# Earlier weights, shorter setup and back-to-back row scatters in a block-sorted attention followed by a routed expert layer

## The chip, the cores and the metric

The kernel runs on one core of one Trainium2 chip. The core has TensorE (PE in the profile; its weight loads are PEld), VectorE (DVE), ScalarE (ACT), GpSimd (POOL) and SyncE (SP), each with its own instruction stream, run in program order. Sixteen DMA engines move data between main memory (HBM) and on-chip memory (SBUF); DMAs are issued here from the POOL queue (software) and the SP queue (hardware). The metric is the device time of one execution in microseconds (us). Before the change it is 233.02 us, the median of three runs (231.26 to 235.55). The profiled execution took 233.46 us, of which the span from the first to the last instruction is 231.7 us.

## The reference

Attention over 4 batches, 8 heads, 768 positions and 64 dimensions. Keys and values are first mixed between 8 blocks of 96 positions by a matrix P (8x8 for each batch and head) that five rounds of row and column normalisation make; each query block attends only to its own sorted block. The output becomes 3072 rows of 512, and every row goes to one of 8 experts, its own best one.

```python
P = sort_net
for _ in range(5):
    P = exp(P - max(P, -1)); P /= sum(P, -1); P /= sum(P, -2)
k_sorted = einsum('bhij,bhjcd->bhicd', P, k_b)      # the same for v
attn = softmax(scale * q_b @ k_sorted_b.T) ; out = attn @ v_sorted_b
x = out.transpose(0, 2, 1, 3).reshape(3072, 512)
logits = x @ w_gate + modality_bias[modality_id]
e_idx = argmax(logits, 1) ; gate_w = softmax(logits)[row, e_idx]
for e in range(8):                                   # w1: 512x1024, w2: 1024x512
    mask = e_idx == e
    out[mask] = gate_w[mask, None] * (relu(x[mask] @ w1[e]) @ w2[e])
```

## The kernel before

The attention is cut into 32 units u = 0 to 31. A unit has one head of a pair of batches (g = u // 16) and half of its blocks. Eight units make a chunk m of 768 rows. When a chunk is complete its rows are gated (`gate_T`, `gate_L`), an expert is chosen for each (`choose`), a place in a scratch tensor in HBM is worked out (`place`, whose first matmuls are called rk in the trace), and eight indirect DMAs of 96 rows each scatter them to that place (`one(t)`). `table(m)` then makes the row addresses of the expert slots of 256 rows that are filled, and the slot's rows are read back, transposed (`xT`), by SP. Slots 0 and 1 become ready with chunk 0, slots 2 and 3 with chunk 1, slots 4 to 7 with chunk 2, slots 8 to 12 with chunk 3. The expert work of a slot is made of "pieces": four of `mL1` (8 matmuls each, hp in the trace) and two of `mL2` (8 matmuls each, yp), whose results leave by an indirect DMA (`y_out`, 25 of them). Even slots use weight buffer 0, odd slots weight buffer 1.

The issue order is fixed by hand. Setup and loads, with cuts:

```python
load_q(0, 0)            # POOL: four heads of q, two DMAs
... iota, identity ...
load_k(0, 0); load_k(0, 1); load_v(0); load_q(0, 1)
spread_q(0, 0, nc.gpsimd); spread_q(0, 1, nc.gpsimd)   # two copies each on POOL
for u in range(4): tq_pe(u)                            # PE transposes of q
...                                                    # five rounds of P; make_bd(0)
for f, g, x0, kd in g0[:8]: f(g, x0, kd)               # sort k of g = 0
scores(0); expo(0)
home_pick(); home_map(); mod_rows()                    # DVE chains, one PE transpose (modT)
load_k(1, 0); load_k(1, 1)
wait_w = gate_consts()                                 # five operations on POOL
make_bd(1)                                             # one PE matmul (rep), three DVE operations
scores(1); expo(1)
late_consts()                                          # eight DVE operations
for n, (f, g, x0, kd) in enumerate(g0[8:]): f(g, x0, kd)   # sort v of g = 0 (va)
load_v(1); load_q(1, 0); load_q(1, 1)
zero_block(); av(0); wait_w(); prep_s(4)
```

The main loop, and what is hung on its units:

```python
at2(9, place, 0)                          # issues scatter 0 of chunk 0
for t in range(1, 8):
    at1(9 + t, lambda t: ones_[0](t), t)  # scatters 1 to 7, one for each unit
    if t == 3: at1(9 + t, lambda: load_w(0, parts=(0,)))
at1(16, table_x, 0)                       # table, then the reads of the slots
at1(16, lambda: load_w(0, parts=(1,))); at1(16, lambda: load_w(1))
at1(18, place, 1) ... at2(24, table_x, 1)
at1(26, place, 2) ... at1(31, table_x, 2)
def pace(u): return (0, 0) if u < 18 else (1, u % 2)   # pieces of a unit
for u in range(2, 32):
    p1, p2 = pace(u)
    scores(u); expo(u)
    for f, a in A1.get(u, []): f(*a)      # at1
    run_pieces(p1)
    av(u - 1); prep_q(u + 2); prep_s(u + 3)
    for f, a in A2.get(u, []): f(*a)      # at2
    run_pieces(p2)
run_pieces(1); av(31); run_pieces(2); gate_T(3, 3); run_pieces(1)
gate_L(3, 3); choose(3); run_pieces(2); place(3)
for t in range(1, 8):
    run_pieces(2); ones_[3](t)
table_x(3); run_pieces(1000)
```

Each scatter after the first of a chunk also waits for the ScalarE or VectorE instruction that `mark[0]` names, so that the rows "leave at an even pace":

```python
ins = nc.gpsimd.indirect_dma_start(out=xs_dram, ...)
after = [mark[0].ins] if t else []
for pre in after:
    tc.add_manual_dep(ins.ins, pre.name, SYNC, reason="rows leave at an even pace")
```

Of the kernel before, what the change touches and what calls it, by code (L numbers as in the profile page):

```python
# [17 lines left out]
def kernel(  # L18
# [72 lines left out]
    def q_in(g, hh):  # L91
        base = q_in1 if g else v_sb[1].rearrange("p x d -> p (x d)")
        return base[:, hh * 3072:(hh + 1) * 3072]
# [19 lines left out]
    def load_v(g):  # L113
        nc.gpsimd.dma_start(out=v_in, in_=v_src[g * 128:(g + 1) * 128])

    def load_q(g, hh):
        t = q_in(g, hh).rearrange("p (r h f) -> p r h f", r=2, h=4)
        return [nc.gpsimd.dma_start(out=t[:, par], in_=q[2 * g + par, 4 * hh:4 * hh + 4]
                                    .rearrange("h (p t) d -> p h (t d)", t=6)) for par in range(2)][0]

    def spread_q(g, hq, eng=None):
        t = q_in(g, hq // 2).rearrange("p (r h t d) -> p r h t d", r=2, h=4, t=6)
        il = q_il[hq % 2].rearrange("p (h t r d) -> p h t r d", h=2, t=6, r=2)
        for z in range(2):
            (eng or nc.vector).tensor_copy(il[:, z], t[:, :, (hq % 2) * 2 + z].rearrange("p r t d -> p t r d"))  # L125
# [1 line left out]
    sI = singles.tile([128, 32], I32)  # L127
    pI = singles.tile([128, 1], I32)
    idI = singles.tile([BLK, NTL], I32)
    load_q(0, 0)  # L130
    nc.gpsimd.iota(sI, pattern=[[1, 32]], base=0, channel_multiplier=0)
    make_identity(nc, ident)
    load_k(0, 0)
    load_k(0, 1)
    load_v(0)
    load_q(0, 1)
    jI = singles.tile([1, 4], I32)
    hI = singles.tile([1, 4], I32)
    nc.gpsimd.iota(pI, pattern=[[0, 1]], base=0, channel_multiplier=1)
# [1 line left out]
    nc.gpsimd.iota(jI, pattern=[[1, 2], [0, 2]], base=0, channel_multiplier=0)  # L141
    nc.gpsimd.iota(hI, pattern=[[PR, 2], [CAP, 2]], base=0, channel_multiplier=0)
    spread_q(0, 0, nc.gpsimd)
    spread_q(0, 1, nc.gpsimd)

    ones_bf = singles.tile([128, 128], BF16)
    ones8 = singles.tile([128, E], FP32)
# [40 lines left out]
    def perm_mult(dst, srcs, nm):  # L188
        eng = nc.gpsimd if nm == "w" else nc.vector
        tmp = small.tile([128, 4, E, E], FP32, tag="ptmp", name=f"ptmp{nm}")  # L190
        a = bass.AP(tensor=srcs.tensor, offset=srcs.offset, ap=[srcs.ap[0], srcs.ap[1], [0, E], srcs.ap[2]])
        p_ = bass.AP(tensor=perm.tensor, offset=perm.offset, ap=[perm.ap[0], [0, 4], perm.ap[1], perm.ap[2]])
        eng.tensor_tensor(tmp, a, p_, ALU.mult)
        return lambda: nc.vector.tensor_reduce(dst, tmp, AX.X, ALU.add)
# [39 lines left out]
    def tq_out(u, eng):  # L234
        g, h = u // 16, u % 8
        qT = qTb[g][:, h * 768:(h + 1) * 768].rearrange("p (i t r) -> p i t r", i=NB, t=6)
        eng(qT, tq.pop(u).rearrange("p t (i r) -> p i t r", r=16))

    for u in range(4):
        tq_pe(u)  # L240
    for it in range(5):
        if it == 0:
            nc.vector.tensor_reduce(red, P_t, AX.X, ALU.max)
            nc.vector.tensor_tensor(P_t, P_t, red.broadcast_to([BH, NB, NB]), ALU.subtract)
        nc.scalar.activation(P_t, P_t, ACT.Exp)
        if it == 3:
            tq_out(0, nc.scalar.copy)
        if it == 4:
            for u in range(1, 4):
                tq_out(u, nc.scalar.copy)  # L250
        for f in gap[it]:
            f()
        nc.vector.tensor_reduce(red, P_t, AX.X, ALU.add)
        nc.vector.reciprocal(red, red)
        nc.vector.tensor_tensor(P_t, P_t, red.broadcast_to([BH, NB, NB]), ALU.mult)
        nc.vector.tensor_reduce(red, P_swap, AX.X, ALU.add)
        nc.vector.reciprocal(red, red)
        colb = bass.AP(tensor=red.tensor, offset=red.offset,
                       ap=[red.ap[0], [0, NB], red.ap[1]])
        nc.vector.tensor_tensor(P_bf if it == 4 else P_t, P_t, colb, ALU.mult)  # L260
# [40 lines left out]

    wgf = small.tile([128, 4, E], FP32, tag="wgf", name="wgf")

    def gate_consts():
        red_w = perm_mult(wgf, wg_sb, "w")
        nc.gpsimd.tensor_scalar(modN, modF, -1.0, 1.0, ALU.mult, ALU.add)

        def bb(r):
            t = BTp[0:BLK, r]
            return bass.AP(tensor=t.tensor, offset=t.offset, ap=[t.ap[0], [0, NTL], t.ap[1]])  # L310
        tmp = small.tile([BLK, NTL, E], FP32, tag="btmp", name="btmp")
        nc.gpsimd.tensor_tensor(biasm, modF.broadcast_to([BLK, NTL, E]), bb(1), ALU.mult)
        nc.gpsimd.tensor_tensor(tmp, modN.broadcast_to([BLK, NTL, E]), bb(0), ALU.mult)
        nc.gpsimd.tensor_tensor(biasm, biasm, tmp, ALU.add)

        def rest_w():
            red_w()
            nc.vector.tensor_copy(wgp, wgf)
        return rest_w

    busy = [0.0, 0.0]

# [54 lines left out]
        return u // 16, (u // 8) % 2, u % 8  # L377

    def prep_s(u):
        if 4 <= u < 32 and not (u // 8) % 2 and u % 2 == 0:  # L380
            spread_q(u // 16, (u % 8) // 2)
            use(dve=0.7)

    def prep_q(u):
        if 4 <= u < 32 and not (u // 8) % 2:
            tq_pe(u)
            tq_out(u, nc.scalar.copy if pick(0.8, 0.56) else nc.vector.tensor_copy)

# [85 lines left out]
    def place(m):  # L474
# [32 lines left out]
        def one(t):  # L507
            if t:
                nc.gpsimd.nop()
            ins = nc.gpsimd.indirect_dma_start(  # L510
                out=xs_dram, out_offset=bass.IndirectOffsetOnAxis(ap=dest[:, t:t + 1], axis=0),
                in_=xt.bitcast(I32)[:, t], in_offset=None)
            after = [mark[0].ins] if t else []
            tc.declare_no_dep(ins.ins, group="xs", reason="rows are disjoint", **({"keep": after} if after else {}))
            tc.add_to_no_dep_group("xs", ins.ins)
            for pre in after:
                tc.add_manual_dep(ins.ins, pre.name, SYNC, reason="rows leave at an even pace")
            scat[m].append(ins.ins)
        ones_[m] = one
        one(0)  # L520
        nxt = ohs[(m + 1) % 2]
        ohsum = small.tile([BLK, E], FP32, tag="ohsum", name=f"ohsum{m}")
        nc.vector.tensor_reduce(ohsum, oh.rearrange("p t e -> p e t"), AX.X, ALU.add)
# [73 lines left out]
    def zero_block():  # L597
        ins = nc.sync.dma_start(out=xs_dram[ZR:ZR + PR].rearrange("(t p) w -> p t w", t=2), in_=zsrc2)
        in_xs_group(ins.ins)
        pads.append(ins.ins)  # L600
# [8 lines left out]
    def w_views(z):  # L609
        o = z * WCOL  # L610
        return (w01[:, o:o + 4 * F].rearrange("p (c f) -> p c f", c=4),
                w01[:, o + 4 * F:o + WCOL].rearrange("p (c f) -> p c f", c=8))

    def load_w(z, tab=None, n=None, parts=(0, 1)):
        tb, n = (etab, z) if tab is None else (tab, n)
        er = nc.values_load(tb[0:1, n:n + 1], engines=(PoolEng,), min_val=0, max_val=E - 1)
        v1, v2 = w_views(z)
        if 0 in parts:
            nc.gpsimd.dma_start(out=v1, in_=moe_w1[bass.ds(er, 1)].rearrange("o (c p) f -> p (o c) f", p=128))
        if 1 in parts:  # L620
            nc.gpsimd.dma_start(out=v2, in_=moe_w2[bass.ds(er, 1)].rearrange("o (c p) f -> p (o c) f", p=128))

    def stage_of(s):
        return 0 if s < 2 else 1 if s < 4 else 2 if s < 8 else 3
# [123 lines left out]
    expo(0)  # L748
    home_pick()
    home_map()  # L750
    mod_rows()
    load_k(1, 0)
    load_k(1, 1)
    wait_w = gate_consts()
    make_bd(1)
    scores(1)
    expo(1)
    late_consts()
    use(dve=-busy[1], act=-busy[0])
    for n, (f, g, x0, kd) in enumerate(g0[8:]):  # L760
        f(g, x0, kd)
    load_v(1)
    load_q(1, 0)
    load_q(1, 1)
    zero_block()
    av(0)
    wait_w()
    prep_s(4)

    st = {"tab": -1, "x": 0, "l1": 0, "done": 0, "pos": 0}  # L770

# [24 lines left out]
    def at2(u, f, *a):  # L796
        A2.setdefault(u, []).append((f, a))

    at2(8, lambda: nc.vector.memset(v_sb[1][:, :, D:D + 1], 1.0))
    for m in range(4):  # L800
        for c in range(4):
# [3 lines left out]
                at2(u, gate_L, m, c)  # L805
        if m < 3:
            at2(8 * m + 9, choose, m)
    at2(9, place, 0)
    for t in range(1, 8):
        at1(9 + t, lambda t: ones_[0](t), t)  # L810
        if t == 3:
            at1(9 + t, lambda: load_w(0, parts=(0,)))
    at1(16, table_x, 0)
    at1(16, lambda: load_w(0, parts=(1,)))
    at1(16, lambda: load_w(1))
    at1(18, place, 1)
    for t in range(1, 8):
        at2(17 + t, lambda t: ones_[1](t), t)
    at2(24, table_x, 1)
    at1(26, place, 2)  # L820
    for t in range(1, 8):
        (at2 if t % 2 else at1)(27 + t // 2, lambda t: ones_[2](t), t)
    at1(31, table_x, 2)
    k_at = [5] * 3 + [6] * 3 + [7] * 3 + [8, 9, 10]
    v_at = [10, 11, 11, 11, 12, 12, 12, 13, 13, 13, 14, 14, 14, 15, 15, 15]
    for u, (f, g, x0, kd) in zip(k_at + v_at, jobs(1, [m_] * 28)):
# [34 lines left out]
    for u in range(2, 32):  # L861
        p1, p2 = pace(u)
        scores(u)
        expo(u)
        for f, a in A1.get(u, []):
            f(*a)
        run_pieces(p1)
        av(u - 1)
        prep_q(u + 2)
        prep_s(u + 3)  # L870
        for f, a in A2.get(u, []):
            f(*a)
        run_pieces(p2)
    run_pieces(1)
    av(31)
    run_pieces(2)
    gate_T(3, 3)
    run_pieces(1)
    gate_L(3, 3)
    choose(3)  # L880
    run_pieces(2)
    place(3)
    for t in range(1, 8):
        run_pieces(2)
        ones_[3](t)
    table_x(3)
    run_pieces(1000)
    assert st["pos"] == len(pieces)
# [74 lines left out]
```

## Time and profile before

| what | before |
|---|---|
| time, median of 3 | 233.02 us |
| span of the profiled execution | 231.7 us |
| busy PE, DVE, ACT, POOL | 164.9, 104.7, 94.3, 76.1 us |
| mean granted TensorE clock | 0.846 |
| last matmul of the expert work starts at | 216.00 us |
| HBM read, written | 27.35, 10.52 MB |

The page has six parts. Its second part cuts the span into 40 slices of 5.8 us and gives the busy share of each engine in tenths, the granted TensorE clock (PEclk) and the DMA share. The chain of waits goes back from the last instruction, at each step to what released it; read forward it is a list of start, length and what was on the path. The list of waits tells which engine stood still for whom: total us, times, longest. A timeline lists one engine's instructions in order of time; in brackets stands the idle time before an instruction and what ended it. A table of windows gives, for stretches of 4 us, the busy us of each engine with its instructions (x), the granted clock (1.00 is full), the DMA share and the GB/s moved.

### The profile page before, as it was taken

The numbers are of one execution on the slowest core, as the hardware profiler recorded it, in microseconds if no ns is written. First come the engines' busy times: TensorE is split into PE (matmuls) and PEld (weight loads), VectorE is DVE, ScalarE is ACT, GpSimd is POOL, SyncE is SP. The second block draws the span as 40 slices with busy tenths as digits, with TensorE's granted clock in tenths as the row PEclk, the third lists the DMA queues.
The fourth block names the chain that finished last, engine by engine and source line by source line (L and its number), as shares of the span: only waits on it lengthen the run. The fifth ranks groups of instructions, "written<-read, shape, count | busy, mean of one in ns | idle before, by whom it ended". The sixth has DMA issues, their size and how long they took to land.

```text
span 231.7 us, 5104 instructions
## 1 busy us (share of the span) xinstructions
PE 164.9 (71%) x2023; PEld 122.8 (53%) x2023; DVE 104.7 (45%) x340; ACT 94.3 (41%) x147; POOL 76.1 (33%) x102
## 2 busy tenths in 40 slices
PE   0265667995999600298889888999990999999600
PEld 0154565985889500286565657668660576674200
DVE  5868866657548660044566436233270133232100
ACT  2264445665577710075464626443341132322300
POOL 7621515000434420031633465337651031333300
PEclk9997587569569955569999999999998699999965
DMA  5999999990119399981215323594364642212200
GB/s 69 208 228 203 218 213 174 198 184 3 36 36 162 101 150 184 191 138 37 108 48 129 97 75 121 127 145 148 96 214 97 105 103 96 92 45 91 89 15 0
DMA packets 30129, 27.67 MB, mean 119 GB/s; under 512 B 18799, under 2 KB 25743, under 8 KB 29840
## 3 DMA queue, kind: packets, MB, share of 16 engines
q0 software_dynamic: 11760, 23.10, 45.7%
q1 hardware_dynamic: 18336, 4.16, 11.8%
q8 instruction: 18, 0.29, 0.6%
q14 instruction: 15, 0.12, 0.2%
HBM read 27.35 MB, written 10.52 MB: 163 GB/s over the span
## 4 chain that ended last, share of the span: by engine, by line
PE 54%; DVE 16%; DMA 13%; issue 5%; POOL 3%; ACT 2%; SPq 1%; POOLq 0%; DVEq 0%
PE hp L663 19%; PE yp L686 15%; DMA xT<-xs_scratch 10%; PE ka L349 3%; PE gt L433 3%; DVE xb L424 3%; PE va L358 3%; PE op L420 3%; PE sc L401 2%; PE lg L439 2%; DMA xs_scratch<-zpad 2%; PE tq L231 1%; POOL xs_scratch L510 1%; DMA xs_scratch<-xb,dest 1%; DVE v_sb L336 1%
## 5 line engine op out<-in xcount | busy, mean ns | idle before, releaser
L663 PE MATMUL hp<-xT,w 128*128 128x256 bf16 x384 | 50.1, 284 | 18.5 <-DMA xT<-xs_scratch 18.4
L510 POOL DMA_INDIRECT xs_scratch<-xb,dest x32 | 29.6, 925 | 68.5 <-issue 33.6
L663 PEld LDWEIGHTS <-w 128*128 128x128 bf16 x384 | 37.6, 102 | 27.1 <-issue 12.6
L677 POOL DMA_INDIRECT out_dram<-kvb,idg x25 | 24.6, 985 | 54.5 <-ACT kvb L673 27.3
L407 ACT ACTIVATE attnT<-sc 96x768 bf16<-96x768 f32 x32 | 25.8, 806 | 10.8 <-PE sc L401 10.6
L657 ACT ACTIVATE hT<-hp 128x512 bf16<-128x512 f32 x17 | 10.1, 596 | 35.7 <-PE hp L663 35.6
L686 PE MATMUL yp<-w,qT 128*128 128x512 bf16 x96 | 22.9, 383 | 0.0
L424 DVE TENSOR_TENSOR xb<-op,rs 96x512 bf16<-96x512 f32 x32 | 22.0, 687 | 1.7 <-DMA xs_scratch<-xb,dest 0.6
L686 PE MATMUL yp<-w,hT 128*128 128x512 bf16 x96 | 22.5, 379 | 0.0
L423 DVE RECIPROCAL rs<-op 96x8 f32<-96x8 f32 x32 | 6.4, 199 | 30.5 <-PE op L420 29.1
L673 ACT ACTIVATE kvb<-yp,idg 128x512 f32<-128x512 f32 x15 | 10.3, 687 | 21.5 <-PE yp L686 21.5
L231 PE MATMUL tq<-ident,q_il 128*128 128x128 bf16 x96 | 10.8, 270 | 10.7 <-POOL q_il L125 10.3
L420 PE MATMUL op<-v_sb,attnT 96*128 96x65 bf16 x256 | 15.1, 207 | 2.1 <-DVE v_sb L336 1.3
L358 PE MATMUL va<-bd,kvb 128*128 128x128 bf16 x128 | 14.6, 285 | 1.4 <-ACT v_sb L336 0.8
L675 DVE TENSOR_SCALAR kvb<-yp,idg 128x512 f32<-128x512 f32 x9 | 6.8, 751 | 19.5 <-PE yp L686 19.5
L401 PE MATMUL sc<-qT,kT 64*128 64x96 bf16 (+1 forms) x256 | 12.9, 228 | 3.0 <-issue 1.1
L420 PEld LDWEIGHTS <-attnT 96*128 96x128 bf16 x256 | 12.8, 107 | 4.2 <-DVE v_sb L336 1.4
L657 ACT ACTIVATE qT<-hp 128x512 bf16<-128x512 f32 x15 | 9.0, 597 | 14.1 <-PE hp L663 14.0
L336 ACT CAST v_sb<-va 96x512 bf16<-96x512 f32 (+1 forms) x20 | 11.9, 629 | 6.7 <-PE va L358 6.5
L433 PE MATMUL gt<-ident,xb 96*128 96x96 bf16 x128 | 9.8, 230 | 6.6 <-DVE xb L424 5.7
L686 PEld LDWEIGHTS <-qT 128*128 128x128 bf16 x96 | 9.3, 100 | 9.5 <-issue 0.5
L358 PEld LDWEIGHTS <-kvb 128*128 128x128 bf16 x128 | 13.2, 189 | 2.0 <-issue 1.8
(176 smaller groups left out, 213.2 us busy)
## 6 DMA issues: line engine op xcount, KB each, us to landing
w<-in_moe_w_dram POOLq DMA_DIRECT2D x4, 1024.0 KB, 15.8
kvb<-in_k_dram POOLq DMA_DIRECT2D x4, 768.0 KB, 12.1
kvb<-in_v_dram POOLq DMA_DIRECT2D x2, 1536.0 KB, 10.7
v_sb<-in_q_dram POOLq DMA_DIRECT2D x4, 384.0 KB, 14.6
q_in<-in_q_dram POOLq DMA_DIRECT2D x4, 384.0 KB, 13.2
xs_scratch<-zpad SPq DMA_DIRECT2D x3, 258.0 KB, 3.4
xs_scratch<-xb,dest POOLq DMA_INDIRECT x32, 2.6
out_dram<-kvb,idg POOLq DMA_INDIRECT x25, 2.9
```

Source lines behind the costliest of these rows:

```text
L336: (nc.scalar.copy if pick(act, dve) else nc.vector.tensor_copy)(dst, src)
L358: nc.tensor.matmul(acc[:, z], v_cols[:, d0 + z], bd[g], start=True, stop=True)
L401: nc.tensor.matmul(sc[0:m, par, j * BLK:(j + 1) * BLK], kT[g][rows, x0:x0 + m], qT[rows, i], start=True, stop=True)
L407: mark[0] = nc.scalar.activation(attnT[u % 2][:, 0:8 * BLK].rearrange("p (r f) -> p r f", r=2), sc_tiles.pop(u)[0:BLK, :, 0:4 * BLK], ACT. ...
L420: nc.tensor.matmul(ov[:, par, j], attnT[u % 2][:, c0:c0 + 128], v_sb[g][0:BLK, par * 64 + h * 8 + i, 0:D + 1], start=True, stop=True)
L424: nc.vector.tensor_tensor(xt[:, :, h * D:(h + 1) * D].rearrange("p (r j) d -> p r j d", r=2), ov[0:BLK, :, :, 0:D], rs.broadcast_to([BLK, ...
L433: nc.tensor.transpose(tp[:, t], xb[m % 2][:, t, c * 128:(c + 1) * 128], ident[:BLK, :BLK])
L510: ins = nc.gpsimd.indirect_dma_start(out=xs_dram, out_offset=bass.IndirectOffsetOnAxis(ap=dest[:, t:t + 1], axis=0), in_=xt.bitcast(I32)[: ...
L657: mark[0] = nc.scalar.activation(dst, src, ACT.Relu)
L663: nc.tensor.matmul(hp[:, f], w_at(s, c * F + (2 * j + f) * 128, 128), xT_b[s % NX][:, c], start=(c == 0), stop=(c == 3))
L677: ins = nc.gpsimd.indirect_dma_start(out=out, out_offset=bass.IndirectOffsetOnAxis(ap=idg[:, t, 0:1], axis=0), in_=y, in_offset=None, boun ...
L686: nc.tensor.matmul(yp, hT_b[s % 2][:, fc, t * 128:(t + 1) * 128], w_at(s, 4 * F + fc * Dm, Dm), start=(fc == 0), stop=(fc == 7))
```

## The change

It has four parts. First, only two heads of q are loaded, spread and transposed before the keys; the other heads follow later, and their spreading goes to POOL for all of the first group. Second, setup that TensorE or VectorE did between scores 0 and the sorting of v (the modality rows, the second block matrix, the late constants, the gate's bias) moves behind it or into units 2 to 4. Third, the weights of buffer 0 are loaded among the q loads of the second group, and those of buffer 1 after the rows of slots 0 and 1 have been read. Fourth, all eight scatters of a chunk are issued in `place`, one after the other without the wait on `mark[0]`, and the table follows in the same unit; in the loop the pieces go ahead of the work hung on the unit, and fewer pieces stand before the last chunk's placing.

```diff
-    load_q(0, 0)
+    load_q(0, 0, 2)
     ...
-    load_q(0, 1)
+    load_q(0, 2, 2)
+    load_q(0, 4, 4)
     ...
-    spread_q(0, 1, nc.gpsimd)
-    for u in range(4):
+    for u in range(2):
         tq_pe(u)
     ...
     def prep_s(u):
-        if 4 <= u < 32 and not (u // 8) % 2 and u % 2 == 0:
+        if 16 <= u < 32 and not (u // 8) % 2 and u % 2 == 0:
     def prep_q(u):
-        if 4 <= u < 32 and not (u // 8) % 2:
+        if 2 <= u < 32 and not (u // 8) % 2:
     ... in place(m):
-            after = [mark[0].ins] if t else []
+            after = []
-        one(0)
+        for t in range(8):
+            one(t)
     ... setup:
-    mod_rows()
     load_k(1, 0)
     load_k(1, 1)
-    wait_w = gate_consts()
-    make_bd(1)
+    wait_w = gate_w()
     scores(1)
     expo(1)
-    late_consts()
     ... sort v of g = 0 ...
+    spread_q(0, 1, nc.gpsimd)
     load_v(1)
-    load_q(1, 0)
-    load_q(1, 1)
+    load_q(1, 0, 4)
+    load_w(0, parts=(0,))
+    load_q(1, 4, 4)
+    load_w(0, parts=(1,))
+    spread_q(0, 2, nc.gpsimd)
     zero_block()
+    prep_q(2)
     av(0)
+    prep_q(3)
     wait_w()
-    prep_s(4)
+    mod_rows()
+    def late_w1():
+        for i, ins in enumerate(load_w(1)):
+            if i == 0:
+                tc.add_manual_dep(ins.ins, xins[1].ins.name, SYNC, reason="rows of the first slots go ahead")
     ... (the lines of chunk 0 to 2 shown above go)
+    at2(2, lambda: (gate_bias(), spread_q(0, 3, nc.gpsimd)))
+    at2(3, make_bd, 1)
+    at2(4, late_consts)
+    at1(10, place, 0)
+    at2(10, table_x, 0)
+    at2(12, late_w1)
     at1(18, place, 1)
+    at2(18, table_x, 1)
     at1(26, place, 2)
+    at2(26, table_x, 2)
     ... main loop:
+        run_pieces(p1)
         for f, a in A1.get(u, []):
             f(*a)
-        run_pieces(p1)
         av(u - 1)
         prep_q(u + 2)
         prep_s(u + 3)
+        run_pieces(p2)
         for f, a in A2.get(u, []):
             f(*a)
-        run_pieces(p2)
     ... after the loop:
-    run_pieces(2)
+    run_pieces(1)
     gate_T(3, 3)
     ...
-    run_pieces(2)
+    run_pieces(1)
     place(3)
-    for t in range(1, 8):
-        run_pieces(2)
-        ones_[3](t)
+    run_pieces(1)
     table_x(3)
```

More of the change, by code (lines that the diff above doesn't have):

```diff
@@ L114, in load_v, with load_q @@
         nc.gpsimd.dma_start(out=v_in, in_=v_src[g * 128:(g + 1) * 128])
[L116 to L119, printed above, removed]
+    def load_q(g, h0, nh):
+        t = q_in(g, h0 // 4).rearrange("p (r h f) -> p r h f", r=2, h=4)
+        z = h0 % 4
+        for par in range(2):
+            nc.gpsimd.dma_start(out=t[:, par, z:z + nh], in_=q[2 * g + par, h0:h0 + nh]
+                                .rearrange("h (p t) d -> p h (t d)", t=6))
     def spread_q(g, hq, eng=None):
@@ L248 @@
         if it == 4:
-            for u in range(1, 4):
-                tq_out(u, nc.scalar.copy)
+            tq_out(1, nc.scalar.copy)
         for f in gap[it]:
@@ L302, with gate_w, rest_w, gate_bias @@
     wgf = small.tile([128, 4, E], FP32, tag="wgf", name="wgf")
-    def gate_consts():
+    def gate_w():
         red_w = perm_mult(wgf, wg_sb, "w")
+        def rest_w():
+            red_w()
+            nc.vector.tensor_copy(wgp, wgf)
+        return rest_w
+    def gate_bias():
         nc.gpsimd.tensor_scalar(modN, modF, -1.0, 1.0, ALU.mult, ALU.add)
@@ L314, in gate_consts @@
         nc.gpsimd.tensor_tensor(biasm, biasm, tmp, ALU.add)
[L316 to L319, printed above, removed]
     busy = [0.0, 0.0]
@@ L617, in load_w @@
         v1, v2 = w_views(z)
+        res = []
         if 0 in parts:
-            nc.gpsimd.dma_start(out=v1, in_=moe_w1[bass.ds(er, 1)].rearrange("o (c p) f -> p (o c) f", p=128))
+            res.append(nc.gpsimd.dma_start(out=v1, in_=moe_w1[bass.ds(er, 1)].rearrange("o (c p) f -> p (o c) f", p=128)))
         if 1 in parts:
-            nc.gpsimd.dma_start(out=v2, in_=moe_w2[bass.ds(er, 1)].rearrange("o (c p) f -> p (o c) f", p=128))
+            res.append(nc.gpsimd.dma_start(out=v2, in_=moe_w2[bass.ds(er, 1)].rearrange("o (c p) f -> p (o c) f", p=128)))
+        return res
     def stage_of(s):
@@ L807 @@
             at2(8 * m + 9, choose, m)
-    at2(9, place, 0)
-    for t in range(1, 8):
[L810 to L815, printed above, removed]
+    at2(2, lambda: (gate_bias(), spread_q(0, 3, nc.gpsimd)))
[4 more added lines that the diff above has]
+    at2(12, late_w1)
     at1(18, place, 1)
-    for t in range(1, 8):
-        at2(17 + t, lambda t: ones_[1](t), t)
-    at2(24, table_x, 1)
+    at2(18, table_x, 1)
     at1(26, place, 2)
-    for t in range(1, 8):
-        (at2 if t % 2 else at1)(27 + t // 2, lambda t: ones_[2](t), t)
-    at1(31, table_x, 2)
+    at2(26, table_x, 2)
     k_at = [5] * 3 + [6] * 3 + [7] * 3 + [8, 9, 10]
@@ L880 @@
     choose(3)
-    run_pieces(2)
+    run_pieces(1)
     place(3)
-    for t in range(1, 8):
-        run_pieces(2)
-        ones_[3](t)
+    run_pieces(1)
     table_x(3)
```

## The prediction

> **What bounds the kernel now.** I read the page first: TensorE is busy for 164.9 of 231.7 us and no other engine comes near it, so the question is where TensorE stands still. The second part of the page shows a hole of two and a half slices in the middle, a small one at three quarters, and slices with a clock of 5 or 6 tenths. Then the list of waits of TensorE (total us, times, longest):
>
> ```profile
> PE hp L663 <- DMA xT<-xs_scratch: 18.4, 2, 12.6
> PE tq L231 <- POOL q_il L125: 10.3, 1, 10.3
> PE gt L433 <- DVE xb L424: 5.7, 6, 1.1
> PE rk L481 <- DVE oh L465: 4.6, 2, 2.9
> ```
>
> The 10.3 us of tq lie in the first 10 us, beside the normalisation of P on VectorE, and set nothing. The other three are real. The chain of waits says what the 18.4 us are:
>
> ```profile
> 77.86 2.68 DMA xs_scratch<-xb,dest
> 80.75 15.98 DMA xT<-xs_scratch
> 96.86 1.87 PE hp L663 x8
> ...
> 171.24 3.82 DMA xs_scratch<-zpad
> 175.19 4.67 DMA xT<-xs_scratch
> 179.91 3.59 PE hp L663 x16
> ```
>
> The first expert matmul waits for a read of 256 rows that takes 15.98 us, where the median of the 13 such reads is 3.4 us. The timeline of POOL shows why:
>
> ```profile
> 77.86 0.91 POOL L510 DMA_INDIRECT xs_scratch<-xb,dest  x1 [2.56 <-ACT attnT L407]
> 78.91 0.94 POOL L621 DMA_DIRECT2D w<-in_moe_w_dram  x1
> 80.10 0.79 POOL L619 DMA_DIRECT2D w<-in_moe_w_dram  x1 [0.25 <-issue]
> 80.89 1.01 POOL L621 DMA_DIRECT2D w<-in_moe_w_dram  x1
> ```
>
> Three weight loads go out around the read and fill the DMA engines; meanwhile, from 52 to 68 us, they had nothing to do. The table of windows (columns: span, busy PE, PEld, DVE, ACT, POOL with counts, clock, DMA share, GB/s):
>
> ```profile
> 52.00:56.00 4.00, 3.21 (x111) 2.81 (x109) 3.00 (x9) 3.08 (x5) 0.00 (x0) 1.00 0.03 7
> 56.00:60.00 4.00, 2.30 (x49) 1.93 (x47) 2.99 (x14) 1.11 (x3) 0.00 (x0) 0.72 0.00 0
> 60.00:64.00 4.00, 3.79 (x57) 3.25 (x56) 2.31 (x6) 2.41 (x4) 2.78 (x3) 0.50 0.21 56
> ...
> 88.00:92.00 4.00, 0.00 (x0) 0.00 (x0) 0.00 (x0) 0.00 (x0) 0.00 (x0) 0.50 1.15 177
> 92.00:96.00 4.00, 0.00 (x0) 0.00 (x0) 0.00 (x0) 0.00 (x0) 0.00 (x0) 0.50 1.20 191
> ```
>
> No compute engine works from 88 to 96 us, and DMA is full.
>
> [...] eight hp matmuls take 1.87 us after the 12.58 us stop and 1.03 later. [...] from 40 to 48 us TensorE is busy throughout and the clock stays at 0.50. [...]
>
> **The change part by part.**
>
> *Start, 0 to 38 us.* Two of four POOL copies (0.82 us each) leave the normalisation of P, where a VectorE multiply took 0.75 us beside them and 0.21 otherwise; this may give half a us at the first matmul of ka (15.57). Sorting v began at 25.66 behind modT and rep. Now scores 1 can follow the exponential of unit 0 (which ends at 23.65), and va can start near 24.1. VectorE is spared make_bd, mod_rows and late_consts between 24.7 and 28.0, so va should end near 30 instead of 33.9. But unit 4's transposes then need spread_q(0, 2), and that now stands on POOL behind v (0.6 us), four q loads (4 x 0.76) and two weight loads (0.8 and 0.95, with a register load of some 0.4 each): 6.2 us after va ends, plus two copies of 0.8, so 38 us. Before, those transposes began at 37.43. I book zero for all this: the gain of 4 us turns into a wait for POOL.
>
> *Units 2 to 17, 38 to 80 us.* The work is the same, with four spreads moved from VectorE to POOL. The wait of rk for chunk 0 (1.70 us) has the key sorting and scores 10 before it now; I book -1 us. In this stretch also fell 0.96 us of gt waiting for VectorE behind the table; -0.5. So unit 18 is reached at about 79 us.
>
> *Rows and weights.* The loads on the POOL ring run at some 215 GB/s until 32 us and 190 after. Before the weights they have 9.44 MB of bf16 to write (3 x 4 x 8 x 768 x 64 x 2 bytes), which ended at about 52 us. The 2.1 MB of buffer 0 add 2.1 / 0.19 = 11 us: done at about 62. Chunk 0's places are known at 59.3 us (as before), eight scatters at the 1.22 us spacing seen in the run from 161.00 to 162.21 take till 70, and the last lands at 73 with 2.7 us. Two reads of 3.4 us: rows of slot 0 at 76.4, of slot 1 at 79. Unit 18 needs slot 0 at 79: the 12.58 us stop is gone, and with it the slow clock behind it (97 to 104 us: five hp groups and their neighbours, about 3.5 us). Buffer 1 is issued at about 80 and needs 11 us, so w1 is there by 87 and w2 by 92; slot 1 starts four units after 18 (at about 92) and its w2 is needed at unit 25 (about 101). It fits with few us to spare. Saved: 12.6 + 3.5 = 16 us, counted from 96.86.
>
> *Units 18 to 31.* A piece (0.88 us of matmuls) now stands between scores and gate_T, which takes up the waits of gt on xb: I count 0.75, 1.09, 0.74, 0.74, 1.09 and 1.06 = 5.5 us after 106 us. The rk of chunk 1 waited 2.86 us; a piece is ahead of it now, so about 1 remains: -2. (This stop lay before 96.86 and is inside the move from 84 to 79.)
>
> *The end.* Before, rk of chunk 3 came at 151.96, the rows of slot 8 at 179.91, 28 us later, and 5.78 us of that was a stop, with 2 us of slow clock after. Now: places 2.3 us after rk, eight scatters 9.8, landing 2.7, read 3.4: 18 to 19 us. The zero rows (3.82 us) wait only for the table, which comes one piece after rk, and are done in time. Between rk and slot 8 stand now 21 pieces, 15 of mL1 (0.88) and 6 of mL2 (1.73): 23.6 us. So the stop goes: -7.8 us.
>
> *Sum.* From 96.86 to the end of the last matmul (217.9) there are 121 us. Less 5.5 (gt), 3.5 and 2 (clock) and 5.8 (stop) leaves 104. From 79 this ends at 183; 1 us of rk makes 184. The tail to the end of the span stays 13.8 us (231.7 - 217.9): 198 us. Packed closer, VectorE and ScalarE (26 and 29 us busy in the 55 us from 97 to 152) will now and then be late: I add 3 us. The time was 1.3 us above the span: 202 us, which is 31 us or 13% less.
>
> **The rivals.** (1) *POOL becomes the gate.* Every load, spread, scatter and output row goes through POOL in order, and the buffer 1 load now waits for the rows of slot 1 in front of chunk 1's scatters. Against it: POOL is busy for 76 us only, with 22 us of pure waiting before the first scatter. For it: spread_q(0, 2) and (0, 3) sit directly on TensorE's path; if each is 3 us later than I think, the time is 206 to 208. (2) *The hole only moves.* If scatters queue behind the weights, or buffer 1 lands after 92, slot 0 or 1 stops TensorE for several us and the clock drops: 5 to 10 us back, 207 to 212. The ring's 190 GB/s in 40 to 52 us speaks against more. (3) *Bursts of eight scatters clog the path of reads and output rows.* Before, five scatters in a row went out at 1.22 us without harm (median landing 2.6 us); the outputs behind have eight buffers. Perhaps 2 us. (4) *The clock is kind.* 40 to 52 and 60 to 68 us ran at half clock; if the shorter stop before rk leaves it at 1.00, about 4 us more are gained: 198.
>
> **Range and chances.** Most of the sum is a stop of 12.6 us whose cause is plain and removed, and one of 5.8 us with 5 us of slack. The upper end takes rivals 1 and 2 in part together (+10), the lower the kind clock and no lateness (-6): 196 to 212. Only if both holes came back at other places would it be within 2% (over 228): 3%. Slower would need a new stop that I don't see: 2%.
>
> **What would show it.** Right: no wait of hp for xT above 2 us; unit 18 at 77 to 81; weights of buffer 0 landed by about 62 and DMA idle no more from 52 to 60; gt waits below 2 us in total; the last matmul near 184 to 187; mean clock above 0.87. The first step to fail would be tq of unit 4 (expected at about 38) or the rows of slot 0 (76). The prediction is wrong if the transposes of unit 4 come after 41 us, or if hp waits for weights.

## The result and the profile after

The changed kernel takes 209.84 us (median of 4 runs, 208.69 to 210.53) against 232.97 us (231.26 to 235.55): a ratio of 0.902, 95% interval 0.895 to 0.910. That lies in the predicted range of 196 to 212, and 7.8 us above the predicted 202.

The list of waits of TensorE in the changed kernel (total us, times, longest) answers to the first fence of the prediction:

```profile
PE tq L233 <- POOL q_il L127: 11.5, 2, 9.6
PE cp L542 <- DVE ohs L528: 3.7, 4, 1.2
...
PE rk L484 <- DVE oh L468: 3.0, 4, 1.1
PE sc L404 <- ACT attnT L410: 1.5, 3, 0.9
```

The 18.4 us that hp waited for xT and the 5.7 us that gt waited for xb are gone from the list. A line is there that was not: cp, the one matmul with which a table begins, waits for the counts (ohs) that VectorE makes at the end of `place`. Of the 11.5 us that tq (the transposes of q) waits, 9.6 again lie beside the normalisation of P; 1.9 are new.

The timeline of POOL shows the scatters of chunk 0 back to back, 1.22 us apart, and the load of buffer 1 released by the read of the rows:

```profile
61.67 1.05 POOL L513 DMA_INDIRECT xs_scratch<-xb,dest  x1 [16.32 <-issue]
63.02 0.93 POOL L513 DMA_INDIRECT xs_scratch<-xb,dest  x1 [0.30 <-issue]
...
70.33 0.93 POOL L513 DMA_INDIRECT xs_scratch<-xb,dest  x1 [0.30 <-issue]
81.34 0.84 POOL L624 DMA_DIRECT2D w<-in_moe_w_dram  x1 [10.08 <-DMA xT<-xs_scratch]
```

The table of windows (columns as in the prediction) shows the DMA engines filled where they were idle, and TensorE at work where it stood:

```profile
52.00:56.00 4.00, 3.21 (x112) 2.80 (x109) 3.07 (x7) 2.62 (x6) 0.00 (x0) 1.00 1.31 202
56.00:60.00 4.00, 2.47 (x63) 2.24 (x61) 3.00 (x12) 2.04 (x4) 0.00 (x0) 0.82 1.24 206
60.00:64.00 4.00, 3.02 (x48) 2.37 (x45) 2.90 (x17) 1.95 (x5) 1.98 (x2) 0.50 0.26 55
...
88.00:92.00 4.00, 3.95 (x54) 2.81 (x53) 1.58 (x5) 3.71 (x6) 3.08 (x4) 1.00 1.15 190
92.00:96.00 4.00, 4.00 (x52) 2.83 (x51) 2.23 (x5) 1.73 (x3) 1.54 (x2) 1.00 1.11 246
```

Where the time came from, by marks of the two timelines:

| mark | before | after | gained so far |
|---|---|---|---|
| first matmul of va | 25.66 | 23.77 | 1.9 |
| tq of unit 4 | 37.43 | 38.50 | -1.1 |
| rk of chunk 0 | 58.00 | 59.15 | -1.2 |
| first expert matmul | 96.86 | 80.98 | 15.9 |
| rk of chunk 3 | 151.96 | 130.86 | 21.1 |
| end of the last matmul | 217.9 | 191.4 | 26.5 |
| end of the span | 231.7 | 206.9 | 24.8 |

Nothing is gained in the first 60 us. 17 us come from the stop in front of the first expert matmul. The next two steps, 5.2 us up to rk of chunk 3 and 5.4 us behind it, have to be read together: two pieces of `mL1` (1.75 us) that stood ahead of this rk before stand behind it now, so about 3.5 us are saved ahead of it and 7.1 us behind it.

### The profile page after: what moved, and what is told of

It is laid out like the page before. It is cut to its first block, busy times and chain, and to the rows that moved or that the text cites. A ratio compares the mean times of both kernels' runs of the same rounds, so it can differ in the third digit from the quotient of the medians.

```text
span 206.9 us, 5081 instructions
## 1 busy us (share of the span) xinstructions
PE 158.8 (77%) x2012; PEld 120.5 (58%) x2023; DVE 104.6 (51%) x339; ACT 92.8 (45%) x144; POOL 80.2 (39%) x108
## 4 chain that ended last, share of the span: by engine, by line
PE 65%; DVE 16%; ACT 4%; issue 4%; POOL 4%; POOLq 0%; DVEq 0%; ACTq 0%
PE yp L692 20%; PE hp L669 19%; PE va L361 5%; PE ka L352 4%; PE sc L404 4%; PE gt L436 3%; PE lg L442 3%; PE op L423 3%; PE tq L233 2%; DVE xb L427 2%; DVE v_sb L339 2%; ACT v_sb L339 1%; DVE xTg L339 1%; ACT attnT L410 1%; DVE P_t L256 1%
## 5 line engine op out<-in xcount | busy, mean ns | idle before, releaser
L669 PE MATMUL hp<-xT,w 128*128 128x256 bf16 x384 | 47.1, 273 | 0.1
L683 POOL DMA_INDIRECT out_dram<-kvb,idg x25 | 24.6, 985 | 48.7 <-ACT kvb L679 23.1
L669 PEld LDWEIGHTS <-w 128*128 128x128 bf16 x384 | 36.2, 98 | 7.3
L679 ACT ACTIVATE kvb<-yp,idg 128x512 f32<-128x512 f32 x14 | 9.6, 688 | 20.9 <-PE yp L692 20.9
L233 PE MATMUL tq<-ident,q_il 128*128 128x128 bf16 x96 | 9.9, 253 | 11.5 <-POOL q_il L127 11.5
L663 ACT ACTIVATE hT<-hp 128x512 bf16<-128x512 f32 x19 | 11.3, 596 | 12.8 <-PE hp L669 12.4
L681 DVE TENSOR_SCALAR kvb<-yp,idg 128x512 f32<-128x512 f32 x10 | 7.5, 750 | 18.8 <-PE yp L692 16.9
L692 PEld LDWEIGHTS <-hT 128*128 128x128 bf16 x96 | 9.1, 98 | 9.1
L663 ACT ACTIVATE qT<-hp 128x512 bf16<-128x512 f32 x14 | 8.4, 597 | 13.3 <-PE hp L669 13.1
L239 ACT COPY qT<-tq 128x768 bf16<-128x768 bf16 x15 | 11.9, 796 | 5.3 <-PE tq L233 5.2
L661 DVE TENSOR_SCALAR qT<-hp 128x512 bf16<-128x512 f32 x10 | 6.9, 692 | 14.3 <-PE hp L669 14.3
L233 PEld LDWEIGHTS <-q_il 128*128 128x128 bf16 x96 | 7.1, 114 | 11.9 <-POOL q_il L127 11.9
## 6 DMA issues: line engine op xcount, KB each, us to landing
w<-in_moe_w_dram POOLq DMA_DIRECT2D x4, 1024.0 KB, 15.9
```

Source lines behind the costliest of these rows:

```text
L233: nc.tensor.transpose(tp[:, t], src[:, t], ident)
L663: mark[0] = nc.scalar.activation(dst, src, ACT.Relu)
L669: nc.tensor.matmul(hp[:, f], w_at(s, c * F + (2 * j + f) * 128, 128), xT_b[s % NX][:, c], start=(c == 0), stop=(c == 3))
L683: ins = nc.gpsimd.indirect_dma_start(out=out, out_offset=bass.IndirectOffsetOnAxis(ap=idg[:, t, 0:1], axis=0), in_=y, in_offset=None, boun ...
L692: nc.tensor.matmul(yp, hT_b[s % 2][:, fc, t * 128:(t + 1) * 128], w_at(s, 4 * F + fc * Dm, Dm), start=(fc == 0), stop=(fc == 7))
```

## The experiments

Each edit is against the changed kernel unless it says otherwise. Theory A is the prediction's account: TensorE's own waits set the time after 80 us, and the two long ones came from rows that were asked for among the weight loads or too late. The runs came in three batches, each with the kernel before beside it:

| run | time, median, us | before in the same batch, us | ratio, 95% interval |
|---|---|---|---|
| changed kernel again | 209.98 | 233.11 | 0.897 (0.892 to 0.903) |
| table later | 203.68 | 233.11 | 0.871 (0.866 to 0.876) |
| spread on VectorE | 208.46 | 233.11 | 0.897 (0.892 to 0.902) |
| paced scatters | 209.09 | 233.11 | 0.893 (0.886 to 0.900) |
| before, early weights alone | 219.08 | 232.19 | 0.947 (0.935 to 0.960) |
| weights late again | 216.36 | 232.19 | 0.941 (0.928 to 0.954) |
| buffer 1 ahead of the rows | 208.92 | 232.19 | 0.903 (0.891 to 0.915) |
| table later and spread on VectorE | 201.53 | 232.19 | 0.873 (0.862 to 0.884) |
| spread on POOL's idle time, table later | 236.43 | 243.76 | 0.969 (0.960 to 0.978) |
| table later and spread on VectorE, again | 236.96 | 243.76 | 0.966 (0.956 to 0.976) |
| old order in the loop | 247.88 | 243.76 | 1.026 (1.018 to 1.035) |
| old place of the setup | 244.40 | 243.76 | 1.014 (1.006 to 1.022) |

The ratio leaves out some of the executions that the medians have, so it is not the quotient of the two medians beside it.

The last four ran where the kernel before itself took 243.76 us and engines stood for many us at waits whose releaser the profile calls only "remote" or "issue" (a wait of VectorE of 9.4 us, for one); the cause is not known. Their times are not compared with the other runs; what is read from their traces is the first 64 us, and for one of them the waits of gt. That this stretch was not disturbed, "old order in the loop" shows: its edit acts only from unit 18 on, which comes later, and its marks in this stretch are those of the changed kernel (va at 23.74 and 23.77 us, tq of unit 4 at 38.47 and 38.50, rk of chunk 0 at 59.18 and 59.15).

**The yardstick.** No edit.

> The changed kernel once more, as the yardstick for the other runs of the same chip: 209 to 210.5 us by either theory.

Measured 209.98 us, as expected.

**Early weights alone, on the kernel before.**

```diff
+    load_w(0, parts=(0,))        # between the two q loads of g = 1
     load_q(1, 1)
+    load_w(0, parts=(1,))
...
-    (the loads in units 12 and 16)
+    at1(16, late_w1)             # buffer 1, after the rows of slot 1
```

> The kernel before with one part of the change alone: weights of buffer 0 among the q loads, those of buffer 1 after the rows of slot 1. Theory A (the early weights are most of the gain): the 12.6 us stop goes, and some 2.5 us of slow clock behind it: 217 to 220 us. Rival (setup and piece order carry it): only 5 us or so are gained, 226 to 229, as the stop shifts to another place.

219.08 us: 13.1 us less than before, as theory A has it. Its chain of waits:

```profile
81.24 3.30 DMA xT<-xs_scratch
84.54 0.14 issue
84.68 1.86 PE hp L665 x8
...
158.58 3.65 DMA xs_scratch<-zpad
...
162.37 4.53 DMA xT<-xs_scratch
...
166.95 3.17 PE hp L665 x14
```

The read is asked for as late as before (81.24 against 80.75) but takes 3.30 us instead of 15.98, so the first stop is gone (0.27 us of 12.58 are left). The slow clock behind it, which theory A expected to go too, stays for the most part: the eight matmuls take 1.86 us (1.03 two groups later), behind a wait of rk of 2.2 us, and from the first hp group to the third it is 5.96 us, before 6.42. The second stop, in front of slot 8, is still there (5.5 us), and so are the 5.7 us of gt: early weights do nothing for these.

**All but the early weights.**

```diff
-    load_w(0, parts=(0,)); ... load_w(0, parts=(1,)); ... at2(12, late_w1)
+    at1(13, lambda: load_w(0, parts=(0,)))
+    at1(16, lambda: load_w(0, parts=(1,)))
+    at1(16, lambda: load_w(1))
```

> The changed kernel with all weight loads back in units 13 and 16 and no wait for rows. Theory A: the rows of slot 0 stand among four weight loads again, hp waits 9 to 13 us for xT, slow clock after it: 220 to 225. Rival: the other parts alone keep most of the gain: 212 to 216.

216.36 us, between the two expectations and nearer the rival's. The five executions spread from 212.06 to 218.43 us, and the profiled one is the fastest of them; in it hp waits 4.5 us, and for the slower ones there is no trace. The chain:

```profile
68.48 2.60 DMA xs_scratch<-xb,dest
...
71.23 14.74 DMA xT<-xs_scratch
...
86.01 1.87 PE hp L669 x8
```

The read is as slow as before (14.74 us), as the four loads were issued from 69.40 to 72.92, around it. But it starts at 71.23 and not 80.75, since table and scatters come early, so most of its length lies beside attention units. The early weights and the early rows are two ways out of the same stop. Alone, the first gains 13.1 us over before and the other parts together 15.8 (232.19 - 216.36); both together gain about 23 and not 29.

The trace also shows what the early weights cost. Without the two loads ahead of the spreading on POOL, tq of unit 4 starts at 36.76 without a wait and rk of chunk 0 at 57.30, 1.9 us earlier than in the changed kernel.

**Paced scatters.**

```diff
+            after = [mark[0].ins] if t else []
-        for t in range(8): one(t)
-    at2(12, late_w1)
+    at2(13, late_w1)
+        one(0)          # one(1) in the same unit, then two in each of three units
+        # the rows are read in the unit of the last one; last chunk: a piece for every second scatter
```

> The eight scatters of a chunk two to a unit, each waiting for the last exponential or relu as before the change, the table where it is, the rows read after the last scatter. Theory A: the burst as such is worth nothing, since rows arrive before TensorE asks for them: 209 to 211, hp waits for xT below 1 us. Rival 1: the burst is what brings rows in time; paced, hp waits for xT again by 3 us or more and the time is 213 or above. Rival 2: bursts disturb loads and output rows; paced is faster by 2 us or more.

209.09 us beside 209.98, and hp does not wait for xT at all. That the scatters touch each other is worth nothing measurable. The pace was quicker than before, though: the eight of chunk 0 start from 61.50 to 72.15 us, in the changed kernel from 61.67 to 70.33, before from 60.53 to 77.86. The old pace with the new table was not run. The queue of SP shows the reads of slot 0 and slot 8, first in the paced kernel:

```profile
74.94 1.36 SPq L635 DMA_TRANSPOSE xT<-xs_scratch  x1
...
147.87 1.86 SPq L635 DMA_TRANSPOSE xT<-xs_scratch  x1
```

and in the changed kernel:

```profile
74.71 1.36 SPq L636 DMA_TRANSPOSE xT<-xs_scratch  x1
...
144.48 1.28 SPq L636 DMA_TRANSPOSE xT<-xs_scratch  x1
```

Paced, the read for slot 8 starts 16.8 us after rk of chunk 3 (131.12), in a burst 13.6 us after it (130.86); both are in time, since TensorE comes to slot 8 some 24.6 us after rk. What both kernels have, and before has not, is a table one piece after the placing and the last scatter at most five pieces after it, where 14 pieces stood before. So that took the second stop away, and not that the scatters touch each other; table and scatters were not moved one by one.

**Buffer 1 ahead of all rows.**

```diff
-    at2(12, late_w1)
+    at2(4, lambda: load_w(1))
```

> The changed kernel with the weights of buffer 1 loaded in unit 4, right behind those of buffer 0 and ahead of all rows. Theory A ([...] 190 to 210 GB/s): loads end near 73 us, the last scatter of chunk 0 lands near 75, rows of slot 0 near 80: hp waits less than 1.5 us, the chunk 1 scatters no longer wait on POOL for the weights: 208.5 to 211. Rival (loads ahead of the rows reopen the stop): hp waits 5 us or more for xT: 215 or above.

208.92 us, and the read of slot 0 starts at 75.12, 0.4 us later than in the changed kernel. Rival 2 of the prediction asks what happens if scatters queue behind the weights. Here the scatters of chunk 0 are issued while the weights of buffer 1 are still landing (208 to 268 GB/s from 60 to 72 us): they take 8.0 us to land (median of the eight; 2.4 in the changed kernel), and POOL stands 2.54 us until a weight load has landed before it issues the eighth at 71.98. Why a scatter takes longer to land there was not shown. But with both buffers loaded by about 72 us hp still does not wait for xT: the rule that rows go ahead of buffer 1 is not needed when the load is this early.

**Table later.** The line cp in the list of waits of the changed kernel asked for this one.

```diff
-    at1(10, place, 0)
-    at2(10, table_x, 0)
+    at2(10, place, 0)
+    at1(11, table_x, 0)         # the same for chunks 1 and 2
...
-    run_pieces(1)
+    run_pieces(2)
     place(3)
-    run_pieces(1)
+    run_pieces(2)
     table_x(3)
```

> Placing moved behind the unit's other TensorE work, the table into the next unit (in the end phase one more piece before each). Theory A: after 81 us TensorE alone sets the time, so the waits of rk and cp behind VectorE (3.0 and 3.7 us in all) are time lost; they fall below 2 us together and the time falls by 3 to 5 us, to 205 to 207. Theory B: these waits only stand where TensorE would soon wait for something else (exponentials, xb, rows); the waits of sc, gt or hp grow and the time stays at 209 to 210.

203.68 us, 6.3 us less than the yardstick, more than theory A's 3 to 5. TensorE's waits from 78 us to its last matmul, first in this kernel:

```profile
PE htl L715 <- ACT xTg L663: 0.5, 1, 0.5
PE sc L404 <- ACT attnT L410: 0.4, 1, 0.4
PE rk L484 <- DVE oh L468: 0.4, 1, 0.4
```

and in the yardstick:

```profile
PE cp L542 <- DVE ohs L528: 2.7, 3, 1.2
PE rk L484 <- DVE oh L468: 2.0, 3, 1.0
PE htl L715 <- ACT xTg L663: 0.5, 1, 0.5
```

4.3 us of waits are gone there, and no other wait has grown in their place by more than 0.1 us: theory B falls. Over the whole span rk and cp fall from 6.3 us together to 1.1. The 6.3 us between the medians are more than these waits. Part of the rest is the clock: the yardstick's trace has 0.85 and 0.72 from 108 to 116 us, behind a wait of cp of 1.17 us, and two hp groups there take 1.84 and 1.41 us; this one has 1.00 there, and its hp groups take 1.05.

**Spread on VectorE, alone and with the table later.**

```diff
-    spread_q(0, 2, nc.gpsimd)
...
+    spread_q(0, 2)               # before wait_w()
-    at2(2, lambda: (gate_bias(), spread_q(0, 3, nc.gpsimd)))
+    at2(2, lambda: (gate_bias(), spread_q(0, 3)))
```

> The spreading of heads 4 to 7 of q on VectorE again, as before the change. Theory A: only the 1.9 us that the transposes of unit 4 wait for POOL come back, so 1 to 2 us less, 208 to 209. Rival (POOL is the gate of the first half): transposes of units 4 and 6 both come 3 us or more earlier and the shift reaches unit 18: 205 to 206. Third possibility: VectorE, which does the copies now, is late elsewhere: 209 to 211.

208.46 us. The ratios to before are equal within their intervals, so the time alone does not settle it; in the trace, tq of unit 4 starts at 37.05 instead of the yardstick's 38.57, and the first expert matmul at 79.28 instead of 81.45. The rival's 205 to 206 is out: the spreading on POOL costs the first half 1.5 to 2.2 us and not 3 or more.

> Table later and spreading on VectorE together. If both waits are TensorE's alone their gains add (their sum in the runs above); if VectorE is the shared cause, the sum is smaller than the parts by 1 us or more.

201.53 us, the lowest median of all. Its last matmul ends at 185.2 us, that of the table alone at 187.3. But the intervals of the two ratios overlap, and the trace of the table alone is of an execution of 204.98 us, above its median. So it is not settled that the pair beats the table alone, nor whether the gains add.

**Spread on POOL's idle time, and the pair again.**

```diff
     spread_q(0, 1, nc.gpsimd)
+    spread_q(0, 2, nc.gpsimd)
     load_v(1)
...
-    spread_q(0, 2, nc.gpsimd)    # with the table later, as above
```

> Table later as in the run of that name, and the spread of heads 4 and 5 on POOL still, but ahead of the load of v, where POOL stood idle for 4 us (28.06 to 32.14 in the trace of the changed kernel). If the wait of unit 4 was one of POOL's order only, its transposes begin near 36 to 37 instead of 38.4, and the time is 201 to 202.5, no worse than with the spreading on VectorE. If POOL's copies cost VectorE time there (it sorts v), va ends later and the time stays near 203.7.

> Table later and spreading on VectorE, beside the run above on the same chip: 201 to 202.5 again.

The times, 236.43 and 236.96 us, tell only that the two are equal there. The traces up to 40 us do answer the question that was put. TensorE's timeline with the spread ahead of the v load:

```profile
35.55 0.62 PE L423 MATMUL op<-v_sb,attnT 96*128 96x65 bf16 x8
35.98 0.83 PE L233 MATMUL tq<-ident,q_il 128*128 128x128 bf16 x6
```

Unit 4's transposes follow without any wait, 2.5 us earlier than in the changed kernel, and va is not later for it (its last matmuls start at 30.59, in the changed kernel at 30.98): the wait was one of POOL's order. What it is worth in the end stays open.

**Old order in the loop.**

```diff
-        run_pieces(p1)
         for f, a in A1.get(u, []): f(*a)
+        run_pieces(p1)
         ...                      # and the same for A2 and p2
```

> The changed kernel with the loop's old order: the work hung on a unit ahead of the piece. Theory A: gt waits for xb again by 4 to 6 us in total and the rk of later chunks loses the piece ahead of it: 214 to 216. Rival: the waits only move from gt to sc or cp: 210 to 212.

247.88 us; what the order alone is worth in time stays open. In its trace gt waits for xb again:

```profile
116.18 0.51 PE L436 MATMUL gt<-ident,xb 96*128 96x96 bf16 x8 [1.06 <-DVE xb L427]
121.92 0.52 PE L436 MATMUL gt<-ident,xb 96*128 96x96 bf16 x8 [1.09 <-DVE xb L427]
```

With a third of 0.73 us these make 2.9 us, fewer than theory A's 4 to 6, but of the lengths that the kernel before has (0.74 to 1.09). The old place of the setup, of the same batch and with the new order, has no such wait. The two runs with the table later have some there (5.1 and 5.3 us in all, up to 3.18 at a time), so the disturbance of this batch makes them too. That the order of the loop took the gt waits away is therefore likely and not shown.

**Old place of the setup.**

```diff
+    mod_rows()
     ...
+    gate_bias(); make_bd(1)      # before scores(1)
     scores(1); expo(1)
+    late_consts()
     ...                          # and their later places go
```

> The changed kernel with the moved setup (modality rows, gate bias, second block matrix, late constants) back ahead of the sorting of v. As predicted, its gain is eaten by the wait for POOL: va starts 2 to 3 us later, the v load and the spreading behind it too, so unit 4 comes 1 to 3 us later and not at the same time: 210 to 213. If it is worth nothing at all: 209 to 210.5.

The time can't be used. Its timeline up to 42 us:

```profile
25.99 2.81 PE L361 MATMUL va<-bd,kvb 128*128 128x128 bf16 x24
...
41.06 0.82 PE L233 MATMUL tq<-ident,q_il 128*128 128x128 bf16 x6 [3.09 <-POOL q_il L127]
```

va starts at 25.99 (23.77 in the changed kernel), tq of unit 4 at 41.06 (38.50), rk of chunk 0 at 61.48 (59.15; 59.18 in the run of the same batch). With POOL's queue as the change orders it, the moved setup is worth 2.3 us at chunk 0.

## Why the prediction was right, and where it was off

The direction and the range held, and so did the main causes: both long stops went, and early weights do remove the first. The last matmul, expected near 184 to 187 us, ended at 191.4. By its own steps:

- *Start, booked at zero.* Nearly right as a sum: rk of chunk 0 comes 1.2 us later than before. Of its parts, va was expected near 24.1 (23.77) and tq of unit 4 at 38 (38.50). That the second is so close is partly luck: va was to end near 30 and ended at 31.8, and POOL then needed 6.7 us and not the 7.8 of the sum. The old place of the setup shows what the zero is made of: the longer POOL queue ahead of the spreading costs, the setup moved away gains about 2.3 us, and they nearly cancel. The half us at ka did not come (15.80 against 15.57): a VectorE multiply still took 1.31 us beside POOL's two copies, where the other four of its line took 0.21.
- *Unit 18 at 79.* 80.70. I had booked 1 us saved at rk of chunk 0. It still waited 1.05 us, and cp, which I had not thought of, 0.98 us.
- *Weights of buffer 0 at 62, rows of slot 0 at 76.4.* The loads end at about 60 us by the windows; the read starts at 74.71, 1.7 us later than I had it. hp waits 0.1 us in all. The stop of 12.58 us was removed by two parts of the change: the early weights alone leave 0.3 us of it, the other parts alone 4.5 us. The prediction gave the credit to the weights.
- *Units 18 to 31, less 5.5 us of gt and the rk of later chunks down to about 1.* This is the mis-sized term. The gt waits on xb did go, all of them. But rk and cp of chunks 1 to 3 wait 4.7 us where I had 1: the table now stands in the unit of its placing, and its matmul comes straight behind VectorE's chain. Moving the table took 6.3 us off the time. The prediction had looked for a new gate on POOL (rival 1) and not on VectorE; the 3 us added for engines that are late now and then cover most of it.
- *Slow clock, less 3.5 and 2.* From the first hp group to the third, 6.42 us before; 6.10 after, of which 1.82 are waits of rk and cp and 0.4 their matmuls, while 0.3 us of lg lie outside: so about 2.2 saved. The 3.5 rested on five slow hp groups; the timeline of before has three in that stretch, and only two are slow (1.87 and 1.70 us; the third takes 1.03). From the start of slot 8 to the end of the last matmul 37.99 and 35.94: 2.05 saved, as expected. Together about 4.2 instead of 5.5.
- *The end, less 5.8 us of stop.* Right: places, scatters and read took 13.6 us from rk to the start of the read (14.8 expected), and slot 8 never waits. That bursts bring this about was not right: paced scatters do as well. The five scatters in a row that rival 3 names were three, with output rows between the others.
- *Tail of 13.8 us.* 15.5 in this trace. In the runs of the first two batches it lies between 13.8 and 15.7, so this is spread and not the change.

Summed on the span of 201 (198 and 3 for late engines): unit 18 with its first expert matmul +2.0, rk and cp +0.7 beyond the 3 and the 1 that were booked, clock +1.3, tail +1.7 make 206.7, where 206.9 was measured.

## What to carry to other kernels

A wait on a read names the read, and the cure can lie on either side of it: take away what it collides with, or ask for it earlier; try both alone before giving one the credit: here their gains did not add (13.1 and 15.8 us alone, about 23 together). When work is moved so that a producer's whole chain stands directly ahead of its consumer, look for the new wait in the list of waits even if the kernel got faster: here moving it away gained another 6 us. Whether the scatters left two to a unit or in a burst mattered nothing (209.09 and 209.98 us), as the rows were there before TensorE asked.

## What was not expected of the hardware

TensorE's clock did not come back soon after TensorE was busy again. In the changed kernel it is busy without a gap from 40 to 52 us, and the windows say:

```profile
40.00:44.00 4.00, 4.00 (x56) 3.58 (x55) 2.84 (x9) 2.29 (x4) 2.83 (x4) 0.50 1.02 189
44.00:48.00 4.00, 4.00 (x78) 3.56 (x76) 2.29 (x12) 3.33 (x5) 0.22 (x1) 0.50 1.25 207
48.00:52.00 4.00, 4.00 (x104) 3.50 (x99) 2.27 (x4) 3.21 (x6) 0.00 (x0) 0.53 1.14 208
```

These 12 us of short matmuls passed at 0.50 to 0.53 before the clock was at 1.00, from 52 to 56 us. It is not a fixed time either: in the yardstick, the same kernel, TensorE works from 38.57 on and the clock is 0.50 from 40 to 44 us and 0.75 from 44 to 48. At rk of chunk 0 the changed kernel stands for 1.05 us, and half clock (0.50) follows from 60 to 68 us. The gap alone does not explain that: with a gap of 0.60 us (table later and spread on VectorE) and with none (spread on POOL's idle time) the clock is 0.50 from 60 to 64 us too. What lowers the clock and what brings it back was not tried.

A 256-row transposed read took 3.30 us with no weight load around it and 14.74 to 21.6 us among weight loads (the 21.6 is that of slot 1 with the weights late again), more than fourfold.
